# Shifting out matmuls by one around four score bursts, and zeroing spare ring rows later, in an attention plus gated-FFN kernel

## The chip, the cores and the metric

The kernel runs on one core of a Trainium2 chip. Times are device microseconds (us) of one execution. "Ratio" below is the mean time of one kernel's fast runs over that of the other's of the same rounds, so it is not quite the ratio of the medians that are quoted beside it. PSUM holds the products of PE until ACT or DVE has read them (the tiles named `_ps`). The span is the profiled execution from its first to its last instruction. The engines are PE (matmul; its weight loads are a lane of their own, PEld), ACT (activation), DVE (vector), POOL (masks here, and the issue of loads) and SP (DMA issue).

## The reference, cut to what matters

```python
# q, k, v: (8 batches, 8 heads, 576, 64); 16 beacon keys and values in front of the 576
scores = q @ concat(beacon_k, k).T / 8       # beacon columns open, the rest causal
a = exp(scores - max); a /= a.sum() + 1e-9
x = (a @ concat(beacon_v, v))                # to (4608 tokens, 512)
out = (gelu(x @ w_gate) * (x @ w_val)) @ w_out   # d_ff = 1536
```

## The kernel before: the parts that matter here

Attention of batch b and the FFN of 512-token chunks alternate. The *out* matmuls of chunk b-1 (48 of them: four row tiles of twelve) are spread through the attention stage of batch b as filler for PE, by calls `o(n)`. A *burst* is a group of three `scores` calls: score matmuls into PSUM, then an exponential (exp) on ACT, then masks on POOL. All scores share three PSUM buffers of pool `psum_s`, which are handed out in turn, so the score number n+3 can only start when exp n has read its buffer.

```python
psum_s: bufs=3      psum_t: bufs=1      psum_o: bufs=1     # out row tiles alternate psum_t, psum_o
...
for r in range(NRING):                       # early, on DVE
    nc.vector.memset(q_ring[r][0:32, 0, :, :], 0.0)
    nc.vector.memset(q_ring[r][64:P, 4, :, :], 0.0)
    nc.vector.memset(k_ring[r][64:P, 4, :, :], 0.0)
...
ahead(5)                                     # first five query loads of batch 2 (POOL queue)
... (batch 0) ...
if b:                                        # attention stage of batch b, exps numbered 1 to 14
    o(4)
    scores(b, (0, 0)); scores(b, (0, 2)); scores(b, (0, 1))            # burst 1: exps 1 2 3
    o(5)
    if b == 1: transpose_pe(1, 3)
    ahead(2)
    o(4)
    scores(b, (0, 3), (1, 3)); scores(b, (1, 0)); scores(b, (1, 2))    # burst 2: exps 4 5 6
    ahead(2)
    o(6)
    av_head(b, 0, 0, psum_t, "t")            # attention @ V of one head, x_ps in psum_t
    o(1)
    scores(b, (1, 1)); scores(b, (2, 0)); scores(b, (2, 2))            # burst 3: exps 7 8 9
    ahead(2)
    av_head(b, 0, 1, psum_t, "t")
    turn_dma(b, 0)
    o(6)                                     # crosses into the third row tile, in psum_t
    scores(b, (2, 1)); scores(b, (2, 3), (3, 3)); scores(b, (3, 0))    # burst 4: exps 10 11 12
    ...
```

(The `scores` calls stand one to a line in the kernel; here they are joined.)

The softmax here doesn't subtract the row's maximum and nothing guards it: scores larger than these inputs give would overflow.

Of the kernel before, what the change touches and what calls it, by code (L numbers as in the profile page):

```python
# [7 lines left out]
P = 128  # L8
# [41 lines left out]
def kernel(  # L50
# [12 lines left out]
    nc = tc.nc  # L63
    keep = tc.keep_in_program_order
# [26 lines left out]
    NRING = 2  # L91
    q_ring, k_ring, v_ring = [], [], []
# [11 lines left out]
    qkT_by_tile = qkT_sb.rearrange("p (w j m c) -> p w j m c", w=2, j=5, m=NPAIR)  # L104
    nc.vector.memset(qkT[:, :, 1, SK:640], 0.0)
    nc.vector.memset(qkT[:, :, 0, 0:NB], 0.0)

    for r in range(NRING):
        nc.vector.memset(q_ring[r][0:32, 0, :, :], 0.0)
        nc.vector.memset(q_ring[r][64:P, 4, :, :], 0.0)  # L110
        nc.vector.memset(k_ring[r][64:P, 4, :, :], 0.0)

    neg = const.tile([P, 256], BF16, name="neg", tag="neg")

# [38 lines left out]
    def load_qk(b):  # L153
        for load in qk_loads(b):
            load()
# [16 lines left out]
    def mm(out_ap, lhsT, rhs, start, stop, **kw):  # L172
        keep(nc.tensor.matmul(out_ap, lhsT, rhs, start=start, stop=stop, **kw))  # L173

    def act(out_ap, in_ap, func, **kw):
        keep(nc.scalar.activation(out_ap, in_ap, func, **kw))  # L176
# [17 lines left out]
    def transpose_pe(b, m, by_act=False):  # L194
        t_ps = psum_s.tile([P, 2, 1024], BF16, name="t_ps", tag="s")
        for w in range(2):
            tr_part(b, m, w, t_ps[:, w, :])
        out_ap = qkT[:, m, :, NB:SK].rearrange("p w (t r) -> p w t r", r=6)
        in_ap = t_ps[:, 0:2, 0:S].rearrange("p w (r t) -> p w t r", r=6)
        keep(nc.vector.tensor_copy(out_ap[:, 1], in_ap[:, 1]))  # L200
        if by_act:
            act(out_ap[:, 0], in_ap[:, 0], ACT.Copy)
        else:
            keep(nc.vector.tensor_copy(out_ap[:, 0], in_ap[:, 0]))  # L204
        keep(nc.vector.tensor_copy(qkT[:, m, 1, 0:NB], t_ps[:, 1, S:SK]))
# [37 lines left out]
    def scores(b, *parts):  # L243
        s_ps = psum_s.tile([P, 2, 512], FP32, name="s_ps", tag="s")
        c0 = 0
        for m, c in parts:
            score_mms(b, m, c, s_ps[:, :, c0 : c0 + CHUNK_W[c]])
            c0 += CHUNK_W[c]
        (m, c), n = parts[0], len(parts)
        o, w = CHUNK_OFF[c], CHUNK_W[c]  # L250
        act(
            exp_ring[:, m : m + n, :, o : o + w].rearrange("p g h c -> p h g c"),
            s_ps[:, :, 0 : n * w].rearrange("p h (g c) -> p h g c", g=n),
            ACT.Exp,
            scale=QK_SCALE,
        )
        if b:
            for m, c in parts:
                masks(b, m, c)
# [87 lines left out]
    def av(b, m):  # L347
        x = psum_s.tile([P, 2, 512], FP32, name="x_ps", tag="s")
        for hi in range(2):
            attend(b, m, hi, x[:, hi, :])  # L350
        normalize(b, m, x, 0, 2)

    def av_head(b, m, hi, pool, tag):
        x = pool.tile([P, 1, 512], FP32, name="x_ps", tag=tag)
        attend(b, m, hi, x[:, 0, :])
        normalize(b, m, x, hi, hi + 1)
# [10 lines left out]
    def turn_dma(b, m):  # L367
        y_sb, y_before = y_of[b * NPAIR + m], y_of.pop((b - 1) * NPAIR + m)
        keep(nc.vector.tensor_copy(y_sb[0:NB, 0, :, :], y_before[KROWS[4] - NB : KROWS[4], 4, :, :]))
        c0 = b * S - NB  # L370
        keep(
            nc.sync.dma_start_transpose(
                out=xT_sb[:, m, c0 : c0 + 5 * P].rearrange("p (j n) -> p j n", n=P),
                in_=y_sb.rearrange("p j e d -> p (j e d)"),
            )
        )
# [3 lines left out]
    def hold(b, m):  # L380
        x = xT_sb[:, m, b * S : (b + 1) * S]
        keep(nc.gpsimd.tensor_copy(hold_sb, x[:, 0 : S : S - 1]))  # L382
# [13 lines left out]
    def gv_mms(ci, fi, *kks, split=False, last=False):  # L396
        if (ci, fi) not in gv_of:
            if split:
                gv_of[ci, fi] = (
                    psum_t.tile([P, CH], FP32, name="g_ps", tag="t"),  # L400
                    psum_s.tile([P, 2, CH], FP32, name="v_ps", tag="s")[:, 0, :],
                )
            else:
                gv_ps = psum_s.tile([P, 2, CH], FP32, name="gv_ps", tag="s")
                gv_of[ci, fi] = (gv_ps[:, 0, :], gv_ps[:, 1, :])
        n0 = ci * CH

        def part(w):
            for kk in kks:
                mm(  # L410
                    gv_of[ci, fi][w],
                    (wg_sb, wv_sb)[w][:, kk, fi * P : (fi + 1) * P],
                    xT_sb[:, kk, n0 : n0 + CH],
                    kk == 0,
                    last and kk == kks[-1],
                    skip_group_check=True,
                )

        part(0)
        if not split:  # L420
            part(1)
        if not last:
            return
        ge_sb = fpool.tile([P, CH], BF16, name="ge_sb", tag="ge_sb")
        act(ge_sb, gv_of[ci, fi][0], ACT.Gelu)
        if split:
            part(1)
        if ci not in h_of:
            h_of[ci] = hpool.tile([P, F_TILES, CH], BF16, name="hT_sb", tag="hT_sb")
        keep(  # L430
            nc.vector.tensor_tensor(  # L431
                out=h_of[ci][:, fi, :], in0=gv_of.pop((ci, fi))[1], in1=ge_sb, op=ALU.mult
            )
        )

    def gate_val(ci, fi, split=False):
        gv_mms(ci, fi, *range(K_CHUNKS), split=split, last=True)
# [27 lines left out]
    def out_mms(ci, u0, u1):  # L465
        for u in range(u0, u1):
            ti, fi = divmod(u, F_TILES)
            if u == 0:
                o_of[ci] = [opool.tile([P, 4, D_MODEL], FP32, name="o_sb", tag="o_sb"), None]
            if fi == 0:  # L470
                o_of[ci][1] = out_ps(ti)
            out_mm(ci, ti, fi, o_of[ci][1])
            if fi == F_TILES - 1:
                out_store(ci, ti, o_of[ci][1])
                if ci >= N_CHUNKS - 2:
                    store(nc.sync)
# [35 lines left out]
    def ahead(n):  # L512
        for load in loads[:n]:
            load()
        del loads[:n]

    ahead(5)

    def c(*parts):
        scores(0, *parts)  # L520

# [40 lines left out]
    for kk in (1, 2, 3):  # L562
        for fi in (0, 1):
            gv_mms(0, fi, kk, last=kk == 3)
    for b in range(B):
        u = [0]

        def o(n):
            out_mms(b - 1, u[0], u[0] + n)
            u[0] += n  # L570

        if b:
            keep(nc.scalar.preload_act_table_set(SET_EXP))
            o(4)
            scores(b, (0, 0))
            scores(b, (0, 2))
            scores(b, (0, 1))
            o(5)
            if b == 1:
                transpose_pe(1, 3)  # L580
            ahead(2)
            o(4)
            scores(b, (0, 3), (1, 3))
            scores(b, (1, 0))
            scores(b, (1, 2))
            ahead(2)
            o(6)
            av_head(b, 0, 0, psum_t, "t")
            o(1)
            scores(b, (1, 1))  # L590
            scores(b, (2, 0))
            scores(b, (2, 2))
            ahead(2)
            av_head(b, 0, 1, psum_t, "t")
            turn_dma(b, 0)
            o(6)
            scores(b, (2, 1))
            scores(b, (2, 3), (3, 3))
            scores(b, (3, 0))
            av_head(b, 1, 0, psum_o, "o")  # L600
            o(5)
            av_head(b, 1, 1, psum_o, "o")
            turn_dma(b, 1)
            scores(b, (3, 1))
            scores(b, (3, 2))
            av(b, 2)
            turn_dma(b, 2)
            o(6)
            av(b, 3)
            turn_dma(b, 3)  # L610
            o(11)
            keep(nc.scalar.preload_act_table_set(SET_GELU))  # L612
            for kk in range(K_CHUNKS):
                for fi in range(2):
                    gv_mms(b, fi, kk, last=kk == 3)
        for fi in range(F_TILES):
            if fi >= 2:
                gate_val(b, fi, fi == F_TILES - 1 and b < B - 1)
            if b == 0 and fi in (6, 7, 9):
                transpose_pe(1, min(fi - 6, 2), by_act=True)  # L620
            if fi == 0:
                if b and b + 1 < B:
                    hold(b, 3)
                    load_v(b + 1)
                if b and b + 2 < B:
                    load_qk(b + 2)
                if 2 <= b + 1 < B:
                    transpose_dma(b + 1)
                store(nc.sync)
# [40 lines left out]
```

## Time and profile before

| | |
|---|---|
| median before | 367.49 us (3 runs), 367.59 us in the run against the change |
| span in the profile | 366.15 us |
| start to first out matmul of batch 1 | 46.50 us |
| batch 1 (first out matmul to first out matmul) | 40.05 us |
| each of batches 2 to 7 | 39.16 us |

The page of the kernel before, busy time (share of the span) and instruction count of each engine, and the summary of the chain that ended last:

```profile
PE 355.5 (97%) x3127; PEld 183.6 (50%) x3170; DVE 154.8 (42%) x305; ACT 188.8 (52%) x243; POOL 161.7 (44%) x288
...
PE 94%; DVE 2%; DMA 1%; issue 1%; POOL 1%; POOLq 0%
```

PE looks full. It is not quite: the recorded length of a 512-column matmul is 379 ns, but in a steady run they start every 216 ns, so a stall of 100 or 160 ns leaves no gap between records. Neither the list of waits nor the busy share shows such a stall. The start-to-start spacing does. These are lines of the timeline of the kernel before, in the attention stage of batch 2 (start us, length us, engine, line, operation, tiles, shape, count, and in brackets the idle time before it and what ended it):

```profile
89.75 1.00 ACT L176 ACTIVATE expT<-s_ps 128x992 bf16<-128x992 f32 x1
90.80 0.38 PE L173 MATMUL s_ps<-qkT 64*128 64x384 bf16 x4
...
94.82 0.49 DVE L339 TENSOR_TENSOR y_sb<-x_ps,r_sb 128x320 bf16<-128x320 f32 x1
95.36 0.39 PE L173 MATMUL o_ps<-wo_sb,hT_sb 128*128 128x512 bf16 x1
...
95.48 0.95 ACT L176 ACTIVATE expT<-s_ps 128x928 bf16<-128x928 f32 x1
96.48 0.39 PE L173 MATMUL s_ps<-qkT 64*128 64x512 bf16 x2
...
88.00 5.37 ACT L176 ACTIVATE expT<-s_ps 128x1024 bf16<-128x1024 f32 x6 [0.22 <-PE s_ps L173]
93.68 3.71 ACT L176 ACTIVATE expT<-s_ps 128x992 bf16<-128x992 f32 x4 [0.31 <-PE s_ps L173]
```

Read the first six lines in pairs. Exp 3 ends at 90.75, and score (1,2), which takes its buffer, starts 0.05 us later, 92 ns over the normal spacing. The normalization of the second head ends at 95.31, and the first out matmul of the third row tile, which takes the same `psum_t` buffer, starts at 95.36, 107 ns late. Exp 9 ends at 96.43, and score (3,0) starts at 96.48, late as well. The last two lines are ACT: it idles 0.22 us before exp 1 and 0.31 us before exp 7, in both cases waiting for PE. So PE and ACT wait for each other in turn. The Trainium skill (Perfetto Trace Analysis, Optimization Strategy) says that the same gap repeating on the engine that should be saturated can mean that there isn't enough PSUM for the next tile; this agrees, with three such gaps in each of six batches.

Two lines of the timeline show what PE waits for in the start:

```profile
6.97 0.39 PE L173 MATMUL s_ps<-qkT 64*128 64x512 bf16 x2 [0.75 <-ACT qkT L176]
...
9.07 0.45 PE L181 MATMUL t_ps<-eye,qk 96*64 96x96 bf16 x12 [0.85 <-DMA qk<-in_q_dram]
```

Both are waits for data, the copy of the first queries by ACT and a query load. The profile names no memset there.

### The profile page before, as it was taken

Reading aid. Unit: us, or ns where it says so; the run is one execution under the profiler, and the core shown is the slowest. Engines: PE = TensorE matmul, PEld = TensorE weight load, DVE = VectorE, ACT = ScalarE, POOL = GpSimd, SP = SyncE. Lnnn points to the kernel's source line nnn. Section 1 sums busy time; section 2 is a strip of 40 time slices with the busy share of each in tenths; the row PEclk is TensorE's granted clock in tenths of the full one; section 3 lists DMA queues with packets and bytes.
Section 4 is the critical chain, followed back from the end, with each engine's and each line's share of the span. In section 5 each row is a group of like instructions: output and inputs, shape, how many; then the busy total and the mean of one; then the engine's idle time right before and its main releaser. Section 6 shows DMA issues by size and latency. Waiting matters only on the chain.

```text
span 366.2 us, 7625 instructions
## 1 busy us (share of the span) xinstructions
PE 355.5 (97%) x3127; PEld 183.6 (50%) x3170; DVE 154.8 (42%) x305; ACT 188.8 (52%) x243; POOL 161.7 (44%) x288
## 2 busy tenths in 40 slices
PE   6899999999999999999999999999999999999996
PEld 6664446444654456444644464445544564444443
DVE  6544545333454335343533354434444353333332
ACT  3973488237933594339723892369334953321210
POOL 8934387565537552845476454656230530000000
PEclk9999999999999999999999999999999999999999
DMA  7999999899069965999299927992795033000103
GB/s 102 172 203 204 197 124 91 135 197 163 20 124 141 213 52 65 163 209 77 56 144 211 122 38 117 170 198 29 100 155 125 11 66 116 0 0 30 57 31 114
DMA packets 160419, 41.57 MB, mean 114 GB/s; under 512 B 146944, under 2 KB 155904, under 8 KB 160384
## 3 DMA queue, kind: packets, MB, share of 16 engines
q0 software_dynamic: 104848, 19.11, 68.9%
q1 hardware_dynamic: 55536, 21.96, 29.7%
q8 instruction: 25, 0.41, 0.5%
q14 instruction: 10, 0.08, 0.1%
HBM read 38.27 MB, written 9.44 MB: 130 GB/s over the span
## 4 chain that ended last, share of the span: by engine, by line
PE 94%; DVE 2%; DMA 1%; issue 1%; POOL 1%; POOLq 0%
PE gv_ps L173 47%; PE o_ps L173 25%; PE x_ps L173 9%; PE s_ps L173 8%; PE v_ps L173 2%; PE g_ps L173 2%; DMA qk<-in_q_dram 1%; PE t_ps L181 1%; DVE qkT L218 1%; POOL qk L116 0%; PE y_ps L181 0%; DVE qkT L200 0%; DVE qkT L204 0%; POOL eye L485 0%; DVE o_sb L450 0%
## 5 line engine op out<-in xcount | busy, mean ns | idle before, releaser
L176 ACT ACTIVATE ge_sb<-gv_ps 128x512 bf16<-128x512 f32 x101 | 59.4, 597 | 142.6 <-PE gv_ps L173 141.5
L431 DVE TENSOR_TENSOR hT_sb<-gv_ps,ge_sb 128x512 bf16<-128x512 f32 x101 | 69.1, 691 | 115.4 <-ACT ge_sb L176 115.4
L173 PE MATMUL gv_ps<-xT_sb,wg_sb 128*128 128x512 bf16 x402 | 111.4, 379 | 0.5
L173 PE MATMUL gv_ps<-xT_sb,wv_sb 128*128 128x512 bf16 x388 | 107.9, 379 | 0.4
L176 ACT ACTIVATE expT<-s_ps 128x992 bf16<-128x992 f32 (+3 forms) x112 | 100.5, 973 | 8.7 <-PE s_ps L173 8.5
L173 PE MATMUL o_ps<-wo_sb,hT_sb 128*128 128x512 bf16 (+2 forms) x420 | 100.6, 373 | 2.1 <-issue 1.1
L303 POOL TENSOR_SCALAR_AFFINE_SELECT expT<-expT 128x256 bf16<-128x256 bf16 (+1 forms) x140 | 52.6, 392 | 53.6 <-ACT expT L176 50.5
L173 PEld LDWEIGHTS <-wv_sb 128*128 128x128 bf16 x432 | 42.2, 98 | 50.6
L173 PEld LDWEIGHTS <-wg_sb 128*128 128x128 bf16 x432 | 42.0, 98 | 50.0
L173 PEld LDWEIGHTS <-hT_sb 128*128 128x128 bf16 x444 | 39.3, 98 | 43.1 <-DVE y_sb L339 3.1
L173 PEld LDWEIGHTS <-expT 128*128 128x128 bf16 (+1 forms) x960 | 33.6, 97 | 9.7 <-DVE y_sb L339 3.1
L450 DVE COPY o_sb<-o_ps 128x512 f32<-128x512 f32 (+2 forms) x37 | 24.9, 672 | 30.3 <-PE o_ps L173 30.2
L173 PE MATMUL x_ps<-v_sb,expT 128*128 128x65 bf16 (+1 forms) x960 | 37.3, 193 | 0.0
L173 PE MATMUL s_ps<-qkT 64*128 64x80 bf16 (+5 forms) x528 | 34.1, 250 | 2.4 <-DVE qkT L222 1.3
L116 POOL DMA_DIRECT2D v_sb<-in_v_dram x40 | 33.7, 860 | 5.9 <-DMA wv_sb<-in_moe_w_val_dram 1.7
L116 POOL DMA_DIRECT2D k_sb<-in_k_dram x30 | 25.2, 846 | 15.9 <-DMA q_sb<-in_q_dram 9.8
L116 POOL DMA_DIRECT2D q_sb<-in_q_dram x30 | 25.4, 876 | 10.3 <-DMA v_sb<-in_v_dram 6.8
L339 DVE TENSOR_TENSOR y_sb<-x_ps,r_sb 128x320 bf16<-128x320 f32 (+1 forms) x47 | 28.8, 612 | 1.6
L337 DVE RECIPROCAL r_sb<-x_ps 128x5 f32<-128x5 f32 (+1 forms) x47 | 9.6, 204 | 45.5 <-PE x_ps L173 45.5
L173 PEld LDWEIGHTS <-qkT 64*128 64x128 bf16 x528 | 17.1, 95 | 18.8 <-issue 12.4
L382 POOL COPY hold_sb<-xT_sb 128x2 bf16<-128x2 bf16 x6 | 1.1, 187 | 31.3 <-DMA xT_sb<-y_sb 31.3
L612 ACT ACT_TABLE_LOAD x7 | 9.0, 1283 | 0.1
(54 smaller groups left out, 116.6 us busy)
## 6 DMA issues: line engine op xcount, KB each, us to landing
out_dram<-o_sb SPq DMA_DIRECT2D x35, 256.0 KB, 7.0
v_sb<-in_v_dram POOLq DMA_DIRECT2D x24, 128.0 KB, 9.0
q_sb<-in_q_dram POOLq DMA_DIRECT2D x18, 128.0 KB, 11.6
k_sb<-in_k_dram POOLq DMA_DIRECT2D x18, 128.0 KB, 5.8
wo_sb<-in_moe_w_out_dram POOLq DMA_DIRECT2D x3, 512.0 KB, 14.4
wg_sb<-in_moe_w_gate_dram POOLq DMA_DIRECT2D x2, 512.0 KB, 11.5
wv_sb<-in_moe_w_val_dram POOLq DMA_DIRECT2D x2, 512.0 KB, 13.2
v_sb<-in_v_dram POOLq DMA_DIRECT2D x8, 112.0 KB, 5.6
```

Of the source, the lines that this page charges most:

```text
L116: keep(nc.gpsimd.dma_start(out=out_ap, in_=in_ap))
L173: keep(nc.tensor.matmul(out_ap, lhsT, rhs, start=start, stop=stop, **kw))
L176: keep(nc.scalar.activation(out_ap, in_ap, func, **kw))
L181: keep(nc.tensor.transpose(out_ap, in_ap, ident[0:n, 0:n]))
L218: keep(nc.vector.tensor_copy(out_ap, in_ap))
L303: nc.gpsimd.affine_select(out=d, in_=d, pattern=[[0, 2], [1, n]], compare_op=ALU.is_ge, fill=0.0, base=0, channel_multiplier=-1,)
L337: keep(nc.vector.reciprocal(r, x[:, :, :, D:DV]))
L339: nc.vector.tensor_tensor(out=y_of[i][:, :, h0:h1, :].rearrange("p j b d -> p b j d"), in0=x[:, :, :, 0:D], in1=r.to_broadcast([P, h1 - h0 ...
L382: keep(nc.gpsimd.tensor_copy(hold_sb, x[:, 0 : S : S - 1]))
L431: nc.vector.tensor_tensor(out=h_of[ci][:, fi, :], in0=gv_of.pop((ci, fi))[1], in1=ge_sb, op=ALU.mult)
L450: keep(nc.vector.tensor_copy(o_sb[:, ti, c0:c1], o_ps))
L612: keep(nc.scalar.preload_act_table_set(SET_GELU))
```

## The change

Its intent is to move bursts 1 and 3 one out matmul earlier, so that ACT starts sooner, and to clear six memsets out of DVE's first microseconds. The loads of batch 2, which write the zeroed rings, have to follow the memsets.

```diff
-    for r in range(NRING):                     # at the start
-        nc.vector.memset(q_ring[r][0:32, 0, :, :], 0.0)
-        nc.vector.memset(q_ring[r][64:P, 4, :, :], 0.0)
-        nc.vector.memset(k_ring[r][64:P, 4, :, :], 0.0)
...
-    ahead(5)                                   # before batch 0
...
+    for r in range(NRING):                     # after the first gated products of batch 0
+        keep(nc.vector.memset(q_ring[r][0:32, 0, :, :], 0.0))
+        keep(nc.vector.memset(q_ring[r][64:P, 4, :, :], 0.0))
+        keep(nc.vector.memset(k_ring[r][64:P, 4, :, :], 0.0))
+    ahead(5)
     for b in range(B):
...
-            o(4)
+            o(3)
             scores(b, (0, 0))                  # burst 1
...
-            o(4)
+            o(5)
             scores(b, (0, 3), (1, 3))          # burst 2
...
-            o(6)
+            o(5)
             av_head(b, 0, 0, psum_t, "t")
...
-            o(6)
+            o(7)
             scores(b, (2, 1))                  # burst 4
```

## The prediction

> **What bounds it now.** The page shows PE (TensorE matmul) busy 97%, and the chain that ended last is 94% PE; ACT is at 52%, DVE 42%. The Trainium skill (Perfetto Trace Analysis, Identifying the Most-Contended Engine) warns that matmul occupancy is no measure of what is left; this trace agrees: matmul records of 379 ns start every 216 ns, so small stalls hide under the recorded ends. I therefore read start-to-start spacing in the timeline. Batches 2 to 7 repeat every 39.15 us. In the attention stage of batch 2 (86.5 to 105 us), over the normal spacing, PE loses:
> - 92 ns before score (1,2) at 90.80, which starts 0.05 us after exp 3 ends (90.75) and frees its PSUM buffer;
> - 107 ns before the first out matmul of the third row tile (95.36), which waits for the normalization of the second head-0 `x_ps` (ends 95.31) in the shared PSUM buffer;
> - 148 ns before score (3,0) at 96.48, waiting for exp 9 (ends 96.43).
> ACT itself idles 0.22 us before exp 1 (table load done at 87.79, first score done later), 0.31 before exp 7, 0.33 before exp 13. Batch 1 loses 0.28 us at score (1,2), waiting for DVE copies of `t_ps` (end 51.72).
>
> **What changes.** The 48 out matmuls of a stage stay 48; bursts 1 and 3 come one out matmul (0.216 us) earlier, bursts 2 and 4 stay; o(7) puts 5 instead of 4 out matmuls before the row-tile switch. Otherwise the order on PE, ACT, POOL and SP is the same. Six DVE memsets (0.27 us each) leave the window 1.7 to 3.7 us and come after the second gated product of batch 0, about 28.3 us.
>
> **Costing, batches 2 to 7.** Burst 1 earlier: exps 1 to 3 start about 0.18 us earlier; exp 3 ends near 90.57, so the 92 ns wait goes. Exp 4 depends on burst 2's own score and stays. Burst 3 comes 0.216+0.092=0.308 earlier; exps 7 to 9 too. But score (2,2) then needs exp 6's buffer (exp 6 ends at 93.37, unchanged): a new wait of about 0.10 us. The extra out matmul covers the 107 ns wait (about 0.10 gained). Burst 4 gains about 0.11, and exp 9 now ends near 96.12, so the 148 ns wait goes. Net about 0.26 us a batch, 1.6 us for six.
> **Batch 1**: transposes come 0.216 earlier, so the wait at (1,2) shrinks by that; with the other waits about 0.4 us (estimate).
> **Start**: nothing, perhaps 0.1. PE waits there for q/k loads (0.9 us at 9.07) and the ACT copy (6.97), not for the memsets.
> **Memsets at 28 us**: they delay two or three gated products by at most 1 us (third: 29.20 to about 30.2). Its PSUM buffer is wanted at 31.83, free near 30.9: no cost. The batch-2 loads issue at 43.91 anyway.
>
> **Predicted**: 367.49 - 2.0 = 365.5 us, 8-in-10 range 364.8 to 366.6. Faster by over 2%: 0.01; within 2%: 0.98; slower: 0.01.
>
> **What would show it.** Period of batches 2 to 7 falls from 39.15 to about 38.9; no gap before (1,2), the third row tile, (3,0); a new gap of about 0.1 before (2,2); ACT idle before exps 1 and 7 shrinks; first 9 us unchanged; PE unbroken at 26 to 33 us.
>
> **What would make it wrong.** Stalls tied to something else (mask ends on POOL), so waits reappear at the attention matmuls; memsets slowing POOL's load issues; the start turning out to hang on DVE.

## More of the kernel before

One fixed cost is not a wait: between 128-row and 64-row matmuls (out and scores) PE loses 94 to 97 ns over the normal spacing each time. The skill (TensorEngine Tiling (Array Packing), Key Properties) says that changing the tiling mode drains the engine; a loss at every such switch agrees with that, and the change leaves the number of switches alone.

## The result, and the profile after

The changed kernel took 366.0 us (median of 6, 365.2 to 366.35) against 367.59 us (367.24 to 368.21): ratio 0.9953, 95% interval 0.994 to 0.9967. The profiled span is 364.43 us, 1.73 us less. From the starts of the first out matmul of each batch in the two timelines:

| | before | after | difference |
|---|---|---|---|
| start to batch 1 | 46.50 | 46.47 | -0.03 |
| batch 1 | 40.05 | 40.04 | -0.01 |
| each of batches 2 to 7 | 39.156 | 38.877 | -0.28, six times: -1.68 |

The three rows sum to -1.72 of the -1.73. (Batch 7 is read from the rest of the span, 83.82 against 83.54 us.)

The page after, in the same two lines as above:

```profile
PE 354.3 (97%) x3127; PEld 184.6 (51%) x3170; DVE 155.4 (43%) x305; ACT 189.0 (52%) x243; POOL 161.2 (44%) x288
...
PE 94%; issue 1%; DMA 1%; DVE 1%; POOL 1%; POOLq 0%; DVEq 0%
```

The page tells nearly nothing of the gain: PE is 97% busy in both. The timeline of the changed kernel in batch 2 tells it:

```profile
87.75 2.75 ACT L171 ACTIVATE expT<-s_ps 128x1024 bf16<-128x1024 f32 x3
90.71 5.35 ACT L171 ACTIVATE expT<-s_ps 128x832 bf16<-128x832 f32 x6 [0.21 <-PE s_ps L168]
96.25 1.00 ACT L171 ACTIVATE expT<-s_ps 128x992 bf16<-128x992 f32 x1 [0.19 <-PE s_ps L168]
...
94.58 0.49 DVE L334 TENSOR_TENSOR y_sb<-x_ps,r_sb 128x320 bf16<-128x320 f32 x1
95.01 0.59 PE L168 MATMUL o_ps<-wo_sb,hT_sb 128*128 128x512 bf16 x2
...
92.37 0.95 ACT L171 ACTIVATE expT<-s_ps 128x928 bf16<-128x928 f32 x1
93.38 0.37 PE L168 MATMUL s_ps<-qkT 64*128 64x384 bf16 x4
...
89.50 1.00 ACT L171 ACTIVATE expT<-s_ps 128x992 bf16<-128x992 f32 x1
90.44 0.58 PE L168 MATMUL s_ps<-qkT 64*128 64x512 bf16 x6
...
95.11 0.95 ACT L171 ACTIVATE expT<-s_ps 128x928 bf16<-128x928 f32 x1
96.13 0.41 PE L168 MATMUL s_ps<-qkT 64*128 64x80 bf16 x4
```

The idle time before exp 1 and exp 7 is gone; what is left in this stretch is 0.21 us before exp 4 and 0.19 before exp 10. The normalization ends at 95.07, and the out matmuls at 95.01 and 0.216 later run through the row-tile switch without a gap. The pair after that is the new wait that the prediction named: exp 6 ends at 93.33, score (2,2) starts at 93.38, 115 ns over the normal spacing. The waits before (1,2) and (3,0) are gone, as the last two pairs show: exp 3 ends at 90.50, and (1,2), within the row at 90.44, starts at 90.66, 214 ns after the matmuls before it; exp 9 ends at 96.06, and (3,0), within the row at 96.13, starts at 96.17, 32 ns after the ones before it.

The sizes add up: 92, 107 and 170 ns saved and 115 lost make 254. Most of the remaining 26 ns to the measured 280 are spacings of some 10 ns that come just after the waits of the kernel before.

The memsets ran where they were expected (timeline of the changed kernel, first, last and next instruction):

```profile
28.29 0.27 DVE L559 MEMSET q_sb<- 32x256 uint32 x1
...
29.98 0.27 DVE L561 MEMSET k_sb<- 64x256 uint32 x1
30.28 1.31 DVE L426 TENSOR_TENSOR hT_sb<-gv_ps,ge_sb 128x512 bf16<-128x512 f32 x2
```

The third gated product starts at 30.28 instead of 29.20 and the fourth at 30.90 instead of 30.93, so one product was late and DVE had caught up by the next; PE shows no gap there.

Batch 1 gained nothing. Here are lines of its timeline in the changed kernel:

```profile
47.09 0.69 DVE L426 TENSOR_TENSOR hT_sb<-v_ps,ge_sb 128x512 bf16<-128x512 f32 x1 [0.82 <-PE v_ps L168]
47.84 0.35 PE L168 MATMUL s_ps<-qkT 64*128 64x80 bf16 x4
...
58.71 0.73 POOL L111 DMA_DIRECT2D k_sb<-in_k_dram  x1
59.81 1.05 POOL L298 TENSOR_SCALAR_AFFINE_SELECT expT<-expT 80x160 bf16<-80x160 bf16 x3
60.55 0.33 PE L168 MATMUL x_ps<-v_sb,expT 128*128 128x65 bf16 x5
```

The last gated product of batch 0 ends at 47.79 and frees the PSUM buffer for score (0,1), which starts at 47.84, 205 ns over the spacing: burst 1 came earlier and then waited for it. At 60.55 the attention of head pair 2 restarts about 0.2 us late, 0.05 us after POOL finished the mask of score (2,3) (60.09 to 60.50); that mask stood behind the issue of two key loads, the last at 58.71. The wait of 278 ns before score (1,2) fell to 64, as predicted, the wait at the third row tile (107 ns) went, and that before (3,0) fell from 118 to 22. So about 0.42 us were saved, and 0.40 given back in two new places.

### The profile page after: what moved, and what is told of

The parts are those of the page before. It is cut to its first block, busy times and chain, and to the rows that moved or that the text cites. A ratio compares the mean times of both kernels' runs of the same rounds, so it can differ in the third digit from the quotient of the medians.

```text
span 364.4 us, 7627 instructions
## 1 busy us (share of the span) xinstructions
PE 354.3 (97%) x3127; PEld 184.6 (51%) x3170; DVE 155.4 (43%) x305; ACT 189.0 (52%) x243; POOL 161.2 (44%) x288
## 4 chain that ended last, share of the span: by engine, by line
PE 94%; issue 1%; DMA 1%; DVE 1%; POOL 1%; POOLq 0%; DVEq 0%
PE gv_ps L168 48%; PE o_ps L168 25%; PE x_ps L168 9%; PE s_ps L168 8%; PE v_ps L168 2%; PE g_ps L168 2%; DMA qk<-in_q_dram 1%; PE t_ps L176 1%; DVE qkT L213 1%; POOL qk L111 0%; PE y_ps L176 0%; DVE hT_sb L426 0%; POOL eye L480 0%; DVE o_sb L445 0%; DVE qkT L217 0%
## 5 line engine op out<-in xcount | busy, mean ns | idle before, releaser
L168 PE MATMUL s_ps<-qkT 64*128 64x80 bf16 (+5 forms) x528 | 33.1, 250 | 2.3 <-DVE qkT L217 1.3
L111 POOL DMA_DIRECT2D k_sb<-in_beacon_k_dram x6 | 3.2, 534 | 13.4 <-DMA v_sb<-in_v_dram 13.4
```

Source lines behind the costliest of these rows:

```text
L111: keep(nc.gpsimd.dma_start(out=out_ap, in_=in_ap))
L168: keep(nc.tensor.matmul(out_ap, lhsT, rhs, start=start, stop=stop, **kw))
```

## The experiments

Kernels are compared only within the same rounds. "Period" is the length of each of batches 2 to 7 in the timeline, repeated within 0.01 us in each profile. It is a far sharper measure than the whole time, because the start (first 46 us) varies from run to run, as the three profiles of the changed kernel show (below).

### The shift alone

```diff
 kernel before, memsets and ahead(5) left in place
-            o(4) ... o(4) ... o(6) ... o(6)
+            o(3) ... o(5) ... o(5) ... o(7)
```

> Only the four counts of out matmuls change; memsets and loads stay where the kernel before has them. Theory (the time comes from PSUM-buffer waits inside the attention stages): as the full change, period of batches 2 to 7 about 38.88 us against 39.16, ratio to before 0.9953 (within 0.001). Rival (clearing DVE at the start or moving the loads gives part of it): clearly less, ratio 0.997 or more, period nearer 39.0.

Measured: 366.05 us against 367.53, ratio 0.9957 (0.9942 to 0.9971); period 38.877 us, batch 1 40.05 us. The counts alone give the change.

### The memsets and loads alone, twice

```diff
 kernel after
-            o(3) ... o(5) ... o(5) ... o(7)
+            o(4) ... o(4) ... o(6) ... o(6)
```

> Only the memsets and the loads of batch 2 move; counts as before. Theory: nothing, ratio 0.9995 to 1.0005, period 39.16 us, first out matmul of batch 1 within 0.05 us of before's 46.50. Rival: 0.5 us or more is gained here, in the first 46 us.

> The memsets and loads alone once more, with more rounds. Theory: nothing, ratio within 0.001 of 1. Rival: clearing DVE at the start gives a little, ratio 0.998.

Measured: 367.85 us against 367.53, ratio 1.0002 (0.9987 to 1.0017); again, with five rounds, 367.48 against 367.70, ratio 0.9993 (0.9972 to 1.0013). The period is 39.156 us both times and batch 1 40.05 and 40.07. The first out matmul of batch 1 came at 45.97 and at 45.29 us, not within 0.05 of before's 46.50, so this part of the first expectation missed. It is not an effect of the memsets, as far as the runs can tell: the unchanged "after" kernel had 46.47, 45.31 and 45.93 in three profiles. An effect of 0.1% of the whole can't be excluded by the intervals.

### Burst 1 alone, burst 3 alone

```diff
 burst 1 alone: kernel before                 burst 3 alone: kernel before
-            o(4)   # before burst 1          -            o(6)   # before av_head(b, 0, 0)
+            o(3)                             +            o(5)
-            o(4)   # before burst 2          -            o(6)   # before burst 4
+            o(5)                             +            o(7)
```

> Only burst 1 comes one out matmul earlier (3, 5, 5, then 6, 1, 6 as before). Theory: the 92 ns wait before score (1,2) goes, the waits before the third row tile (107 ns) and before score (3,0) (about 148 ns) stay, because exp 7 moves only with burst 3; period 39.16 - 0.09 = 39.07 us, total about 0.6 us less, ratio 0.9985. Rival (starting the exps earlier is what saves): most of the 0.28 us a batch, period near 38.9.

> Only burst 3 comes one out matmul earlier and o(7) follows (4, 5, 4, then 5, 1, 7). Theory: the 92 ns before (1,2) stay; the third-row-tile wait goes; exp 7 to 9 come 0.216 us earlier, so score (3,0) waits about 0.03 instead of 0.15; score (2,2) waits at most 0.02. Period 39.16 - 0.22 = 38.94 us, total about 1.4 us less, ratio 0.996. Rival (exps 1 to 3 earlier is what saves): period stays near 39.1.

Measured: burst 1 alone 367.08 us, ratio 0.9982 (0.9967 to 0.9997), period 39.05 us, so -0.106 a batch. The wait before (1,2) is gone; those at the third row tile (110 ns) and before (3,0) (about 166 ns) stand. Burst 3 alone 366.46 us, ratio 0.9959 (0.9943 to 0.9976), period 38.94 us, so -0.216 a batch. The 92 ns before (1,2) stand, the row-tile wait is gone, the wait before (3,0) is down to about 50 ns, and (2,2) waits for nothing. The rival, that starting the first exps earlier is the main thing, falls: that half gives a third of the gain.

Each half saves what it was expected to save, to within 0.02 us a batch. The halves sum to 0.322 us and together give 0.28: together they make the wait of 115 ns before (2,2), which neither makes alone, and in return the last 50 ns before (3,0) go. (That leaves about 0.02 us of the difference unexplained.)

The two runs also part the terms of batch 1. With burst 1 alone it takes 40.06 us: a wait of 208 ns before score (0,1) comes and the one before (1,2) shrinks by as much. With burst 3 alone it takes 39.87 us, 0.19 less than before, and neither of the two new waits is there. So the move of burst 1 gains nothing in batch 1, and of these kernels the wait for the late masks appears only in those with both moves.

In batch 2 the waits that stand show as before, as a score that starts 0.05 us after its exp: (3,0) after exp 9 with burst 1 alone, and (1,2) after exp 3 with burst 3 alone:

```profile
94.81 0.95 ACT L176 ACTIVATE expT<-s_ps 128x928 bf16<-128x928 f32 x1
95.81 0.39 PE L173 MATMUL s_ps<-qkT 64*128 64x512 bf16 x2
```

```profile
89.59 1.00 ACT L176 ACTIVATE expT<-s_ps 128x992 bf16<-128x992 f32 x1
90.64 0.38 PE L173 MATMUL s_ps<-qkT 64*128 64x384 bf16 x4
```

There the timeline of burst 3 alone shows ACT without a gap from exp 4 to exp 10, and burst 1 alone still has its gap before exp 7:

```profile
90.60 6.54 ACT L176 ACTIVATE expT<-s_ps 128x832 bf16<-128x832 f32 x7
```

```profile
90.20 2.62 ACT L176 ACTIVATE expT<-s_ps 128x832 bf16<-128x832 f32 x3 [0.21 <-PE s_ps L173]
93.01 4.47 ACT L176 ACTIVATE expT<-s_ps 128x992 bf16<-128x992 f32 x5 [0.20 <-PE s_ps L173]
```

### Batch 1 relieved of its two waits

```diff
 kernel after
-            o(3)                     # before burst 1
+            o(4 if b == 1 else 3)
-            o(5)                     # before the transposes
+            o(4 if b == 1 else 5)
             scores(b, (2, 2))
-            ahead(2)
+            if b > 1:
+                ahead(2)
...
             scores(b, (3, 2))        # burst 5
+            ahead(2)
```

> The changed kernel, with batch 1 alone treated otherwise: 4 and 4 out matmuls before the transposes, and the last two key loads issued after burst 5. Theory: in batch 1 the shift is given back by two waits of PE, 0.205 us before score (0,1) (its PSUM buffer waits for the last gated product of batch 0) and 0.197 us inside the attention of pair 2 (masks queued on POOL behind load issues); both go, so batch 1 takes about 39.65 us instead of 40.04 and the total is about 0.4 us below the changed kernel (ratio to before about 0.994). Rival (batch 1 is bound by something else, such as the DVE copies of its transposes): batch 1 stays at 40.0.

Measured: 367.34 us, ratio 0.9986 (0.9946 to 1.0027), batch 1 41.03 us: slower by 1 us instead of faster by 0.4. Both waits did go. The first gate matmul after the attention of batch 1 that the two timelines share comes at 66.26 instead of 66.65 us, that is 0.41 earlier counted from the first out matmul (46.49 and 46.47). But then PE stood still. From the waits of this run (total us, times, longest):

```profile
PE gv_ps L168 <- DMA xT_sb<-y_sb: 1.2, 1, 1.2
```

It waited for a transpose of attention output by DMA. In the chain of this run (start us, length us) that transpose is:

```profile
62.38 6.11 DMA xT_sb<-y_sb
```

In the changed kernel the same transpose was issued at 62.78 and landed after 4.2 us. The moved key loads were issued at 62.05 and 62.93, around it. In 64 to 66 us (window view: stretch, length, busy time of PE, PEld, DVE, ACT and POOL, granted clock, DMA share, GB/s), first this run, then the changed kernel:

```profile
64.00:66.00 2.00, 2.00 (x11) 0.88 (x9) 0.89 (x3) 0.00 (x0) 0.00 (x0) 1.00 2.17 130
```

```profile
64.00:66.00 2.00, 2.00 (x11) 0.88 (x9) 0.89 (x3) 0.00 (x0) 0.00 (x0) 1.00 0.44 88
```

PE did the same work, but the DMA engines were five times as busy. So the waits were rightly named, and the mending collided with a transfer that batch 1 needed soon. The move of the loads brought this wait: the version below has the same counts in batch 1 with the loads left in place, and the wait is absent there. That the loads held the transpose up by contention for the DMA engines is read from these lines, and not tested by moving the loads to a third place.

### Other scores in bursts 1 and 2

```diff
 kernel after
             scores(b, (0, 2))
-            scores(b, (0, 1))        # 992 wide
+            scores(b, (0, 3), (1, 3))   # 832 wide
...
-            o(5)
-            scores(b, (0, 3), (1, 3))
+            o(4)
+            scores(b, (0, 1))
             scores(b, (1, 0))
             scores(b, (1, 2))
...
-            o(5)
+            o(6)
             av_head(b, 0, 0, psum_t, "t")
```

> The changed kernel, with scores (0,3),(1,3) (832 wide) in burst 1 and (0,1) (992 wide) in burst 2, and burst 2 one out matmul earlier. Theory: the new wait of 0.115 us before score (2,2) comes from exp 6 ending at the same time as before; here exp 3 ends about 0.13 us and exp 6 about 0.1 us earlier, so the wait goes: period about 38.77 to 38.8 us against 38.88, total about 0.5 us below the changed kernel. Rival (the wait before (2,2) is not exp 6, or it reappears before (1,2) or (3,0)): period 38.86 to 38.9.

> Both of the two variants before. Theory: the gains add, about 0.8 us below the changed kernel (ratio to before about 0.993); batch 1 keeps its own counts. If they do not add, batch 1 with the swapped chunks waits somewhere new.

> The changed kernel itself again, as the yardstick on this chip for the three variants: ratio to before 0.9953 within 0.001, period 38.88 us.

Measured: with the swap 365.62 us, ratio 0.9954 (0.9901 to 1.0006); period 38.83 us, batch 1 40.15 us. With both variants 366.81 us, ratio 0.9976 (0.9927 to 1.0025); period 38.83, batch 1 41.26. The changed kernel again, on that chip: 365.72 us, ratio 0.9941 (0.9899 to 0.9982); period 38.877, batch 1 40.05. The intervals are wide: one run of the kernel before took 370.32 us at a granted clock of 0.986, and one of the swap 368.05 at 0.985. By the period, the swap gives 0.05 us a batch of the expected 0.08 to 0.11. The wait before (2,2) fell from 115 to 32 ns. So exp 6 was its cause. The expectation that the wait goes entirely missed: 32 ns stay there and some 22 come back before (3,0), which is part of what the rival said. In batch 1 the swap lost 0.1 us, which was not followed up. The combination fails for the reason of the batch 1 run: its list of waits has the same 1.2 us for `xT_sb`.

### Both mendings, with the loads left alone

```diff
 kernel after, with the swap for b > 1 only, and for b == 1 only:
-            o(3) ... o(5) before the transposes
+            o(4) ... o(4) before the transposes      # load issues left alone
```

> The changed kernel with the swapped chunks in batches 2 to 7 only, and in batch 1 the old chunks with 4 and 4 out matmuls before the transposes; load issues as in the changed kernel. Theory: period 38.83 us as in the run with the swap, and batch 1 loses the wait before (0,1) of 0.205 us without the late load that broke the earlier fix: batch 1 at 39.85 us, total about 0.5 us below the changed kernel. Rival: the wait for masks in batch 1 takes the 0.2 back, batch 1 at 40.0.

> The changed kernel again, for the comparison with the variant on the same chip: ratio to before 0.995, period 38.88 us; its first out matmul of batch 1 anywhere from 45.3 to 46.5 us, as the first two profiles of this same kernel had it.

Measured: 365.26 us (364.79 to 366.41, 6 runs), ratio to before 0.9937 (0.9916 to 0.9957); period 38.83 us, batch 1 39.84 us. The changed kernel beside it: 365.83 us (365.30 to 366.01), ratio 0.9945 (0.9925 to 0.9964), period 38.88, batch 1 40.08. In the timelines that is 0.24 us in batch 1 and 0.05 in each of six more, 0.5 us in all, and the medians differ by 0.57; but the ranges of the times overlap, so the whole time alone doesn't prove it. The mask wait in batch 1 (194 ns here) stays, since the loads stay. In batch 2 ACT has no gap left between exp 1 and exp 11:

```profile
86.28 1.28 ACT L571 ACT_TABLE_LOAD   x1
87.57 10.12 ACT L171 ACTIVATE expT<-s_ps 128x1024 bf16<-128x1024 f32 x11
```

So moving out matmuls can gain little more in this stretch: the exps follow each other from the table load on, and what is left waits for an exp (score (3,0) of batch 2 is still 72 ns late).

Three profiles of the changed kernel differ by 1.16 us in the start alone (46.47, 45.31, 45.93). In the second, the wait for the query load below is absent from the list of waits; in the first, the timeline has it:

```profile
9.00 0.45 PE L176 MATMUL t_ps<-eye,qk 96*64 96x96 bf16 x12 [0.63 <-DMA qk<-in_q_dram]
```

### Why the last gated product of batch 0 starts late

```diff
 kernel after
-    ahead(5)                          # at the end of batch 0
...
                 transpose_pe(1, 3)
+                ahead(5)
             ahead(2)
```

> The changed kernel with the five query loads of batch 2 issued only after the transposes of batch 1, so that POOL issues no load while DVE makes the last gated product of batch 0. Question: why that product starts 0.47 us after its wait ended, in every profile, when in the other batches it takes 0.07. If POOL's load issue holds DVE up, it starts 0.07 us after the wait here; if it is DVE's own (something that comes with this place in the program), 0.47 stays. The total will be worse, by a microsecond or more, since masks of batch 1 queue behind the loads.

Measured: one look, 371.56 us (state unknown), worse as expected, by more than 5 us. The product still started 0.484 us after the semaphore instruction before it (45.48 to 45.96), with POOL idle from 41.3 to 47.7 us. POOL's load issue is not the reason. In the later batches the same step takes 0.07 us, and in batch 0 it took 0.47 to 0.48 in every profile that was read for it. What holds DVE up there stays open. Lines of this run's timeline, DVE, and of its windows:

```profile
45.96 0.69 DVE L426 TENSOR_TENSOR hT_sb<-v_ps,ge_sb 128x512 bf16<-128x512 f32 x1 [0.83 <-PE v_ps L168]
```

```profile
57.00:61.00 4.00, 3.78 (x30) 0.50 1.29 82
```

The second line (stretch, PE busy, granted clock, DMA share, GB/s) is a lesson beside the question. The masks that queued behind the loads held PE up for 3.8 us (52.25 to 56.08); the granted clock was 0.50 from 55.35 to 62.18, and out matmuls started every 427 ns. The skill (TensorE: Matmul & The Clock Gate, Part 1) says that PE falls back to half its clock after an idle window of about 3.4 us; this run roughly agrees, with the fall 3.1 us after the last matmul had started.

## Why the prediction was right

The prediction was 365.5 us in 364.8 to 366.6; measured were 366.0, 365.72 and 365.83 us.

1. *Three waits a batch, all for PSUM buffers.* Right. Each went (the one before (3,0) but for 50 ns) in the run that was to remove it and stood in the other (burst 1 alone, burst 3 alone).
2. *Net 0.26 us a batch for batches 2 to 7.* Right: 0.28. The period fell from 39.16 to 38.88 ("about 38.9"). The wait before (3,0) was some 20 ns longer than the 148 of the sum.
3. *A new wait of about 0.10 us before (2,2).* Right: 115 ns, directly behind exp 6. The swap made exp 6 earlier and the wait fell to 32 ns.
4. *Batch 1: about 0.4 us.* Wrong, and this is where the sum was mis-sized: 0.01 us. The step that failed was "transposes come 0.216 earlier, so the wait at (1,2) shrinks by that; with the other waits about 0.4 us". The wait at (1,2) did shrink. But I took the end of batch 0 to be like the end of other batches. The last gated product of batch 0 starts 0.4 us later after its semaphore than elsewhere, in the kernel before as well, where nothing waited for it by then (0.4 us sooner it would have freed the buffer at 47.39, before score (0,1) was due at 47.63); and POOL in batch 1 issues loads between masks. The first took 0.205 back and the second about 0.2; the run that removed both reached the end of the attention 0.41 us sooner. The late product and the loads between the masks stood in the profile before. With counts of its own batch 1 does gain 0.2 (39.84).
5. *Memsets and start: nothing.* Right within the noise: ratios 1.0002 and 0.9993, one product late by 1.1 us and no gap on PE.
6. *First 9 us unchanged.* Can't be judged: PE waits for the copy and the load there in the changed kernel too, but the same kernel differs by over 1 us from run to run in the start.

Without the batch 1 term the arithmetic gives 367.49 - 1.6 = 365.9 us, close to what was measured. The range of 1.8 us was wide enough to hold the error of 0.4, so a time inside it says nothing for the batch 1 term.

## What to carry to other kernels

When a full engine is 97% busy, compare start-to-start spacing with that of an undisturbed stretch, and look for a release just before each late start (0.05 us here): that suggests the buffer, and moving one burst at a time tests it. Moving filler work by one instruction was worth about the wait that it removed here, until the next buffer in the ring took over, so follow every move through one whole cycle of the ring, and do it separately for the first round, whose neighbours differ. Before moving a load out of a queue's way, look what transfers run where it lands: a load moved by 4 us turned 0.4 us won into 1 us lost.

## What the Trainium skill lacked or had wrong

- TensorE: Matmul & The Clock Gate, Back-to-back issue gap, gives a sustained 131 ns per matmul for 512 columns in a stream of weight loads and matmuls, and calls 216 ns the isolated figure. In this kernel's streams, with a weight load for each, 512-column matmuls start every 215 to 216 ns at the full granted clock. (Elsewhere the same page has 216 for back-to-back matmuls too; it is the 131 that these runs don't bear out.)
- TensorEngine Tiling (Array Packing), Key Properties, says that a mode switch drains the engine but not what it costs: 94 to 97 ns over the normal spacing, each way, between the 128-row out matmuls and the 64-row score matmuls here.
- No page that I found says how soon a matmul follows the release of its PSUM buffer: 0.05 us after the recorded end of the exp or product (90.75 to 90.80, 95.31 to 95.36, 93.33 to 93.38 here).
- No page that I found explains a vector instruction that starts 0.47 to 0.48 us after the semaphore instruction before it at one place of a program, and 0.07 us at all like places; the runs leave it open.
